# Signs of weights from scaled words in PSUM, and a pair's maxima split in PSUM

## The chip, the cores and the metric

The kernel runs on one core of one Trainium2 chip. The metric is device time in microseconds (us), the median of several runs. TensorE (PE) multiplies, VectorE (DVE), ScalarE (ACT) and GpSimd (POOL) do elementwise work, SyncE (SP) and ACT issue DMAs. Each engine works through its own instructions in order; semaphores order the engines among each other. SBUF is the working memory, PSUM the memory that matmuls write to, in eight banks.

## The reference

```
mask   = (q_bucket[..., :, None] == k_bucket[..., None, :])     # buckets: six sign bits of q @ proj, k @ proj
scores = where(mask, (q @ k.T) / 8, -1e9)                        # 2 batches x 8 heads, 768 x 768, head_dim 64
attn   = exp(scores - max(scores)); attn /= (sum(attn) + 1e-9)
x      = (attn @ v), heads joined: 1536 tokens x 512
h      = x @ w_in;  x = (s * relu(h)**2 + b) @ w_out             # first layer, 512 -> 2048 -> 512
h      = x @ w_in2; out = (h * clip(h + 3, 0, 6) / 6) @ w_out2   # second layer
```

All inputs are float32. The kernel receives the four weight matrices as 64-bit words (each float widened to a double, read as two 32-bit words), and makes float32 words of them on the chip.

## The kernel before, in words

The queries are cut into four units (two batches, two halves of 384 queries), each with four pairs of heads: 16 pairs, numbered g. For a pair, `qk` makes six tiles of scores twice (128 queries against 384 keys), and `smax` (line 473, DVE) reduces each to its negated row maximum, in two columns per slot. Masking is part of the product: key bits scaled by 2^100 push pairs of different buckets far down, so a row without any partner shows a maximum beyond 2^99. `both` (line 477) joins the two halves, `nx_split` (lines 483 to 486) clears such rows, adds a constant, splits the sum into a high and a low part and makes a flag, all into columns of `cols`; `nx_mm` (line 491, PE) transposes `cols` through a PSUM bank; `rows_in` (line 497, DVE) writes the rows into QA; `u_rows` (line 502, ACT) copies the rows with the flags out of the same bank. Then `st` makes the transposed scores with the maxima included, `texp` their exponentials, `t_hi` and `t_lo` (ACT, POOL) split these into two halves of 16 bits, `pv_mm`, `den_mm`, `recip`, `r_mm`, `x_scale`, `x_hi` and `x_lo` give the pair's part of x. Keys and queries are split in the same way (`k_hi` on ACT; `k_lo`, line 358, on POOL).

The two layers are eight jobs, one per layer and unit. A job has 32 weight tiles of 128x512: 16 for the first product (whose results pass `g_relu`, `g_prod`, `g_hi` and `g_lo` into G), 16 for the second. Each tile is split into a high part (`w_hi`, line 658, ACT) and a low part (`w_lo`, line 664, POOL), and takes 12 matmuls (line 688).

The first job of each layer also converts the weights, tile by tile: `w_load` brings 128x1024 words; `w_exp` (line 624, ACT) scales the upper words by 2^-112 into a PSUM bank, `wm`; `w_ends` with half 0 (line 636, ACT) writes the lower 16 bits of the new words, with half 1 (line 638, DVE) their upper 16 bits, which are the sign alone; `w_join` (line 643, DVE) shifts the scaled words left by three and joins them in. Then the tile is stored for the later jobs of the layer. The two conversions run from about 80 to 250 us and from about 360 to 463 us; attention of later pairs runs beside them.

The order on every engine comes from a planner (class `Plan`): each step is added with an engine, a due time, an estimated duration, what it needs, and which buffers of which ring it takes and gives back. The planner goes forward through the steps and picks, on each engine, the one that is due first among those that can start. A step's estimate or a ring's holder that changes can change the whole order. Rings that matter here: `S` with two PSUM banks (score tiles, and from pair 4 on the small products of a pair, that of `nx_mm` among them), `mm` with one PSUM bank (`wm`, and the small products of pairs 0 to 3).

Of the kernel before, what the change touches and what calls it, by code (L numbers as in the profile page):

```python
# [8 lines left out]
F32 = mybir.dt.float32  # L9
F32R = mybir.dt.float32r  # L10
# [11 lines left out]
NQ = 384  # L22
# [204 lines left out]
def attn_moe_moe2(ctx, tc, qT, kT, vT, proj, cvec, eye, w1_in, w1_out, w2_in, w2_out, out):  # L227
# [48 lines left out]
    cols = [const.tile([128, 114], F32R, name=f"cols{e}") for e in range(2)]  # L276
# [192 lines left out]
    def smax(s, j):  # L469
        g, c = divmod(s, SPP)  # L470
        if c == 0 and j == 0:
            pd[g]["nh"] = sm_p.tile([128, 2, SPP], F32, tag="nh", name="nh")
        nc.vector.reduce_max(out=pd[g]["nh"][:, j, c:c + 1], in_=sd.pop((s, j))[:, 0:NQ], axis=AX.X, negate=True)  # L473

    def both(g):
        pd[g]["nx"] = sm_p.tile([128, SPP], F32, tag="nx", name="nx")
        nc.vector.tensor_tensor(out=pd[g]["nx"], in0=pd[g]["nh"][:, 0], in1=pd[g]["nh"][:, 1], op=ALU.min)

    def nx_split(g):

# [256 lines left out]
    def o_store(j, d, key):  # L737
# [7 lines left out]
                 "vt": 4, "iv": 4, "pvs": 1, "U": 1, "ds": 1, "kH": 1, "qD": 1, "kHx": 1, "qDx": 1, "nx": 3, "nh": 2, "cols": 2, "fl": 1,  # L745
# [37 lines left out]
    for g in range(NP):  # L783
# [85 lines left out]
    for jn, (m, j, n) in enumerate(jobs):  # L869
        t0, dt = M[jn]  # L870
        prev = [("mm", jn - 1, 28 + f // 4) if jn else None for f in range(16)]
        for i in range(32):
            key = (jn, i)
            t = t0 + i * dt
            if jn == first[m]:
# [5 lines left out]
                    rel=[(wr, ck, 3)])  # L881
# [3 lines left out]
                add("DVE", tw, 0.66, w_join, (ck,), needs=[("we",) + ck, ("wd", 1) + ck], gives=[("wf",) + ck],  # L885
# [100 lines left out]
```

## Time and profile before

| | |
|---|---|
| runs | 907.68, 904.6, 899.4 us; median 904.6 |
| profiled execution | 901.18 us; span from first to last instruction 899.3 us, mean granted clock 0.971 |
| PE matmul / weight load, busy | 836.7 us (93%) / 741.4 us (82%) |
| DVE, ACT, POOL, busy | 497.8 us (55%), 590.5 us (66%), 574.5 us (64%) |
| the chain that ended last | PE 78%, DVE 12%, ACT 3%, DMA 3% |

Busy shares are means over stages that differ. The chain is followed back from the last instruction: at each step to what released it, or to the instruction before it on its engine. A wait of PE for DVE names the line that came last. "Granted clock" is the share of TensorE's full speed that the chip granted in a stretch.

### The profile page before, as it was taken

The numbers are of one execution on the slowest core, as the hardware profiler recorded it, in microseconds if no ns is written. First come the engines' busy times: TensorE is split into PE (matmuls) and PEld (weight loads), VectorE is DVE, ScalarE is ACT, GpSimd is POOL, SyncE is SP. The second block draws the span as 40 slices with busy tenths as digits, with TensorE's granted clock in tenths as the row PEclk, the third lists the DMA queues.
The fourth block names the chain that finished last, engine by engine and source line by source line (L and its number), as shares of the span: only waits on it lengthen the run. The fifth ranks groups of instructions, "written<-read, shape, count | busy, mean of one in ns | idle before, by whom it ended". The sixth has DMA issues, their size and how long they took to land.

```text
span 899.3 us, 15265 instructions
## 1 busy us (share of the span) xinstructions
PE 836.7 (93%) x5430; PEld 741.4 (82%) x5430; DVE 497.8 (55%) x852; ACT 590.5 (66%) x993; POOL 574.5 (64%) x388
## 2 busy tenths in 40 slices
PE   6689889779999999988999999999999999999998
PEld 2456569568887889977978997999998788999998
DVE  8577777887757673789544433540465542530520
ACT  4368769696875963899876636663588464753752
POOL 5467645684786856455778658566588665665664
PEclk9688899898999999999999999999999999999999
DMA  8858443566557666878966443444334222444442
GB/s 191 139 99 241 115 134 123 178 194 206 191 168 190 145 157 163 259 246 257 284 201 180 130 123 92 144 129 122 114 103 117 77 65 86 125 128 122 128 139 74
DMA packets 74988, 136.73 MB, mean 152 GB/s; under 512 B 20288, under 2 KB 30880, under 8 KB 74912
## 3 DMA queue, kind: packets, MB, share of 16 engines
q1 hardware_dynamic: 73088, 132.15, 51.4%
q10 hardware_dynamic: 1824, 3.60, 1.8%
q8 instruction: 43, 0.70, 0.3%
q14 instruction: 33, 0.27, 0.1%
HBM read 103.86 MB, written 21.54 MB: 139 GB/s over the span
## 4 chain that ended last, share of the span: by engine, by line
PE 78%; DVE 12%; ACT 3%; DMA 3%; issue 2%; SPq 0%; DVEq 0%; ACTq 0%
PE mm L688 55%; PE T L525 6%; PE S L465 6%; PE pv L554 5%; DVE wf L638 2%; DVE nh L473 2%; PE S L565 2%; DMA KA<-bits 1%; PE pv L586 1%; PE S L381 1%; DVE wf L643 1%; ACT P L531 1%; DVE QA L497 1%; DMA qD<-q_t 1%; PE pv L374 1%
## 5 line engine op out<-in xcount | busy, mean ns | idle before, releaser
L664 POOL TENSOR_TENSOR wl<-wf,wh 128x512 fp32r<-128x512 f32 x256 | 331.3, 1296 | 218.3 <-ACT wh L658 187.0
L688 PE MATMUL mm<-G,wh 128*128 128x384 f32 x1024 | 270.8, 346 | 6.2 <-DVE G L720 4.8
L688 PE MATMUL mm<-X,wh 128*128 128x384 f32 x1024 | 265.0, 339 | 10.7 <-DVE G L723 6.1
L658 ACT CAST wh<-wf 128x512 fp32r<-128x512 f32 x256 | 158.3, 618 | 111.1 <-PE mm L688 70.7
L544 POOL TENSOR_TENSOR pt<-P,pt 128x768 f16<-128x768 f32 x96 | 160.1, 1671 | 69.4 <-ACT pt L538 62.8
L688 PEld LDWEIGHTS mm<-X,wh 128*128 128x128 f32 x1024 | 183.1, 188 | 22.4 <-DVE G L723 9.8
L688 PEld LDWEIGHTS mm<-G,wh 128*128 128x128 f32 x1024 | 184.6, 190 | 18.5 <-issue 11.0
L688 PE MATMUL mm<-G,wl 128*128 128x384 f32 x512 | 173.8, 339 | 0.3 <-POOL wl L664 0.3
L688 PE MATMUL mm<-X,wl 128*128 128x384 f32 x512 | 171.8, 336 | 0.0
L473 DVE TENSOR_REDUCE nh<-S 128x1 f32<-128x384 f32 x192 | 104.2, 552 | 84.3 <-PE S L465 83.7
L531 ACT ACTIVATE P<-T 128x768 f32<-128x768 f32 x96 | 77.8, 810 | 39.5 <-PE T L525 34.3
L688 PEld LDWEIGHTS mm<-G,wl 128*128 128x128 f32 x512 | 96.9, 189 | 0.6 <-POOL wl L664 0.6
L688 PEld LDWEIGHTS mm<-X,wl 128*128 128x128 f32 x512 | 96.2, 188 | 0.3 <-POOL wl L664 0.3
L465 PE MATMUL S<-KA,QA 76*128 76x384 f32 x192 | 73.9, 385 | 15.1 <-DVE nh L473 9.1
L538 ACT CAST pt<-P 128x768 f16<-128x768 f32 x96 | 79.8, 834 | 7.4 <-PE pv L554 3.8
L525 PE MATMUL T<-QA,KA 108*128 108x384 f32 x192 | 71.1, 370 | 5.2 <-DVE QA L497 4.9
L525 PE MATMUL T<-QB,KB 128*128 128x384 f32 x192 | 68.7, 358 | 0.0
L465 PE MATMUL S<-KB,QB 128*128 128x384 f32 x192 | 68.0, 354 | 0.0
L465 PEld LDWEIGHTS S<-KA,QA 76*128 76x128 f32 x192 | 38.2, 199 | 31.8 <-DVE nh L473 14.4
L554 PE MATMUL pv<-pt,vt 128*64 128x384 f16 x576 | 61.8, 337 | 1.5 <-POOL pt L544 1.0
L638 DVE TENSOR_SCALAR wf<-wr 128x512 uint16<-128x512 uint16 x64 | 59.3, 926 | 6.5 <-DMA wr<-w_in 5.9
L358 POOL TENSOR_TENSOR KB<-kH,KA 64x1536 fp32r<-64x1536 f32 x14 | 48.8, 3487 | 13.6 <-ACT KA L352 13.4
(356 smaller groups left out, 985.9 us busy)
## 6 DMA issues: line engine op xcount, KB each, us to landing
wf<-w SPq DMA_DIRECT2D x187, 256.0 KB
wr<-w_in SPq DMA_DIRECT2D x32, 512.0 KB
w<-wf SPq DMA_DIRECT2D x64, 256.0 KB
wr<-w_out SPq DMA_DIRECT2D x32, 512.0 KB
KB<-KA SPq DMA_DIRECT2D x15, 384.0 KB
kH<-k_t SPq DMA_DIRECT2D x14, 384.0 KB
qD<-q_t SPq DMA_DIRECT2D x28, 192.0 KB
U<-ur SPq DMA_DIRECT2D x16, 192.0 KB
```

The costliest lines, as they stand in the source:

```text
L358: nc.gpsimd.tensor_tensor(out=operand(g, "KB")[0:64], in0=pd[g]["k"], in1=operand(g, "KA")[0:64].bitcast(F32), op=ALU.subtract)
L465: nc.tensor.matmul(out=sp[:, 0:NQ], lhsT=operand(g, Q)[0:n, h, 128 * t:128 * t + 128], rhs=operand(g, K)[0:n, h, NQ * j:NQ * j + NQ], star ...
L473: nc.vector.reduce_max(out=pd[g]["nh"][:, j, c:c + 1], in_=sd.pop((s, j))[:, 0:NQ], axis=AX.X, negate=True)
L525: nc.tensor.matmul(out=tp[:, j, 0:NQ], lhsT=operand(g, K)[0:n, h, c:c + 128], rhs=operand(g, Q)[0:n, h], start=(a == 0), stop=(a == 1))
L531: nc.scalar.activation(out=P, in_=td.pop((g, k))[:, :, 0:NQ], func=AF.Exp, scale=0.125)
L538: (nc.scalar.copy if THI(g) == "ACT" else nc.vector.tensor_copy)(pd[g][h][:, 0, 2 * i:2 * i + 2], pd[g]["P", k])
L544: e.tensor_tensor(out=pt[:, 1, 2 * i:2 * i + 2], in0=pd[g].pop(("P", k)), in1=pt[:, 0, 2 * i:2 * i + 2], op=ALU.subtract)
L554: nc.tensor.matmul(out=d["pv"][64 * h:64 * h + 64, 0:NQ], lhsT=vt[:, vc, 64 * h:64 * h + 64], rhs=d[h][:, a, c], start=(c == 0 and n == 0) ...
L638: nc.vector.tensor_scalar(out=f16[:, :, 1], in0=r16[:, :, 3], scalar1=0x8000, scalar2=None, op0=ALU.bitwise_and)
L658: nc.scalar.copy(hi.rearrange("p a b -> p (a b)"), wq[key]["wf"])
L664: nc.gpsimd.tensor_tensor(out=lo.rearrange("p a b -> p (a b)"), in0=d["wf"], in1=d["hi"].rearrange("p a b -> p (a b)").bitcast(F32), op=AL ...
L688: nc.tensor.matmul(out=a, lhsT=w[:, k, :], rhs=src[k][:, xi, :], start=(k0 + k == 0 and p == 0), stop=(k0 + k == nk - 1 and p == 2))
```

## The change

The sign is no longer taken from the loaded words in SBUF with a 16-bit instruction. `w_low` (before: `w_ends`, half 0) now writes whole 32-bit words with the lower 16 bits as value; `w_sign` takes the sign bit of the scaled words in PSUM and joins it to them; `w_join` follows. So the sign now needs both ACT instructions, and a loaded tile is given back by ACT alone. For a pair, the maxima go into a fixed buffer of three columns per slot, the third a constant 2^99; one reduction takes the least of the three into PSUM, and two instructions, not five, follow it there in place of `both` and `nx_split`. Rows without a partner are no longer cleared; their flag is made from the transposed rows by `u_rows`, which moves from ACT to DVE. `nx_split` now takes the PSUM bank that `nx_mm` took, and the planner's entries say so.

```diff
-    cols = [const.tile([128, 114], F32R, name=f"cols{e}") for e in range(2)]
+    cols = [const.tile([128, 108], F32R, name=f"cols{e}") for e in range(2)]
+    maxima = [const.tile([128, 3, SPP], F32, name=f"nh{e}") for e in range(2)]
...
-        nc.vector.reduce_max(out=pd[g]["nh"][:, j, c:c + 1], in_=sd.pop((s, j))[:, 0:NQ], axis=AX.X, negate=True)
-
-    def both(g):
-        pd[g]["nx"] = sm_p.tile([128, SPP], F32, tag="nx", name="nx")
-        nc.vector.tensor_tensor(out=pd[g]["nx"], in0=pd[g]["nh"][:, 0], in1=pd[g]["nh"][:, 1], op=ALU.min)
+        nc.vector.reduce_max(out=maxima[g % 2][:, j, c:c + 1], in_=sd.pop((s, j))[:, 0:NQ], axis=AX.X, negate=True)
 
     def nx_split(g):
 
-        nx, c = pd[g]["nx"], cols[g % 2]
-        mk = sm_p.tile([128, SPP], F32, tag="mk", name="mk")
-        nc.vector.scalar_tensor_tensor(out=mk, in0=nx, scalar=2.0 ** 99, in1=nx, op0=ALU.is_lt, op1=ALU.mult)
-        nc.vector.tensor_scalar(out=c[:, 96:102], in0=mk, scalar1=LN, scalar2=None, op0=ALU.add)
-        nc.vector.scalar_tensor_tensor(out=c[:, 102:108], in0=mk, scalar=LN, in1=c[:, 96:102].bitcast(F32), op0=ALU.add, op1=ALU.subtract)
-        nc.vector.tensor_scalar(out=c[:, 108:114], in0=nx, scalar1=2.0 ** 99, scalar2=None, op0=ALU.is_ge)
+
+        t, c = bank(g), cols[g % 2]
+        nx = t[:, 128:128 + SPP]
+        nc.vector.tensor_reduce(out=nx, in_=maxima[g % 2].rearrange("p j s -> p s j"), axis=AX.X, op=ALU.min)
+        nc.vector.tensor_scalar(out=c[:, 96:102], in0=nx, scalar1=LN, scalar2=None, op0=ALU.add)
+        nc.vector.scalar_tensor_tensor(out=c[:, 102:108], in0=nx, scalar=LN, in1=c[:, 96:102].bitcast(F32), op0=ALU.add, op1=ALU.subtract)
+        pd[g]["nr"] = t
...
     def u_rows(g):
         fl = raw_p.tile([128, 128], F32, tag="fl", name="fl")
-        nc.scalar.copy(fl[96:114], pd[g]["nr"][96:114, 0:128])
+        nc.vector.tensor_scalar(out=fl[96:102], in0=pd[g]["nr"][96:102, 0:128], scalar1=2.0 ** 99, scalar2=None, op0=ALU.is_ge)
...
-            nc.scalar.activation(out=f16[:, :, 0], in_=r16[:, :, 1], func=AF.Copy, scale=2.0 ** -13, bias=2.0 ** -14 - 0.5)
-        else:
-            nc.vector.tensor_scalar(out=f16[:, :, 1], in0=r16[:, :, 3], scalar1=0x8000, scalar2=None,
-                                    op0=ALU.bitwise_and)
+    def w_low(key):
...
+        nc.scalar.activation(out=d["wf"], in_=r16[:, :, 1], func=AF.Copy, scale=2.0 ** -13, bias=2.0 ** -14 - 0.5)
+
+    def w_sign(key):
+        d = wq[key]
+        nc.vector.scalar_tensor_tensor(out=d["wf"], in0=d["mt"], scalar=-2147483648, in1=d["wf"], op0=ALU.bitwise_and,
+                                       op1=ALU.bitwise_or)
...
-                for h in range(2):
-                    add("DVE" if h else "ACT", tw, 0.85 if h else 0.67, w_ends, (ck, h), needs=[("wr",) + ck] + ([("wd", 0) + ck] if h else before("wi", jn, i)),
-                        acq=[] if h else [("wf", ck)], gives=[("wd", h) + ck] + ([] if h else [("wi",) + ck]), rel=[(wr, ck, 3)])
+                add("ACT", tw, 0.65, w_low, (ck,), needs=[("wr",) + ck] + before("wi", jn, i),
+                    acq=[("wf", ck)], gives=[("wd",) + ck, ("wi",) + ck], rel=[(wr, ck, 2)])
+                add("DVE", tw, 0.69, w_sign, (ck,), needs=[("we",) + ck, ("wd",) + ck], gives=[("wg",) + ck])
```

The planner then orders everything anew. Three places of the order follow; names and lines are those of each kernel.

On DVE, the split of pair 5 (in the stretch 160 to 172 us of the profile), before and now:

```order
L473 TENSOR_REDUCE nh<-S 128x1 x2
L477 TENSOR_TENSOR nx<-nh 128x6
L705 SCALAR_TENSOR_TENSOR mm<-mm,cv,r__1906 128x384
L483 SCALAR_TENSOR_TENSOR mk<-nx 128x6
L484 TENSOR_SCALAR cols_143<-mk 128x6
L485 SCALAR_TENSOR_TENSOR cols_143<-mk,cols_143 128x6
L486 TENSOR_SCALAR cols_143<-nx 128x6
L638 TENSOR_SCALAR wf<-wr 128x512
L497 TENSOR_TENSOR QA_152<-S,eyes 12x768
L643 SCALAR_TENSOR_TENSOR wf<-wm,wf 128x512
```

```order
L479 TENSOR_REDUCE S<-nh_145 128x6
L480 TENSOR_SCALAR cols_143<-S 128x6
L481 SCALAR_TENSOR_TENSOR cols_143<-S,cols_143 128x6
L631 SCALAR_TENSOR_TENSOR wf<-wm,wf 128x512
L636 SCALAR_TENSOR_TENSOR wf<-wm,wf 128x512
L491 TENSOR_TENSOR QA_154<-S,eyes 12x768
L713 SCALAR_TENSOR_TENSOR G_1382<-mm,cv,G_1382 128x384
L698 SCALAR_TENSOR_TENSOR mm<-mm,cv,r__1887 128x384
L496 TENSOR_SCALAR fl<-S 6x128
```

Five instructions ahead of the transposition have become three (479 to 481), sign and join of a weight tile (631, 636) stand between them and the rows for QA (491), and the flag (496) comes two instructions after these, in the same PSUM tile S.

On ACT, in the conversion of the second matrix (wm: scaled words, r: relu, G: upper half, wh: upper half of a weight tile), before and now:

```order
L636 ACTIVATE wf<-wr 128x512
L624 ACTIVATE wm<-wr 128x512
L714 CAST G_1364<-mm 128x384
L658 CAST wh<-wf 128x512
L699 ACTIVATE r__4536<-mm,three 128x384
L658 CAST wh<-wf 128x512
L636 ACTIVATE wf<-wr 128x512
L624 ACTIVATE wm<-wr 128x512
```

```order
L618 ACTIVATE wm<-wr 128x512
L627 ACTIVATE wf<-wr 128x512
L532 CAST pt<-P 128x768
L692 ACTIVATE r__4511<-mm,three 128x384
L651 CAST wh<-wf 128x512
L618 ACTIVATE wm<-wr 128x512
L707 CAST G_1378<-mm 128x384
L627 ACTIVATE wf<-wr 128x512
L692 ACTIVATE r__4547<-mm,three 128x384
```

The scaling (624, now 618) always followed the low half (636, now 627); now it precedes it in some tiles, directly or with an instruction of G between.

On SP at the start, from the shift of pair 1's keys on (before, ACT issued `KA_151<-bits`, the key bits of pair 1, after the transpose in the planner's order), before and now:

```order
L355 DMA KB_153<-KA_151 64x1536
L342 DMA qD<-q_t 64x2x384 x2
L348 DMA vP<-v_t 128x768
L451 DMA_TRANSPOSE vt<-vhl 128x12x128
L406 DMA QA_152<-bits 12x384 x2
```

```order
L356 DMA KB_155<-KA_153 64x1536
L335 DMA kHx<-k_t 64x1536
L356 DMA KB_162<-KA_160 64x1536
L415 DMA KA_153<-bits 12x384 x4
L403 DMA kb_118<-bits 128x384
L343 DMA qDx<-q_t 64x2x384 x2
L407 DMA QA_154<-bits 12x384 x2
L349 DMA vP<-v_t 128x768
L452 DMA_TRANSPOSE vt<-vhl 128x12x128
```

The key and query bits of pair 1 (KA_153, QA_154) now stand ahead of the first transpose, on SP; two more loads of keys and shifts stand ahead of them.

## Rows read from the trace of the kernel before

**Rows 1.** Busy time by stage: window, length, engines in us (instructions), granted clock, DMA.

```profile
core 0: us, PE busy (x) PEld busy (x) DVE busy (x) ACT busy (x) POOL busy (x), PEclk, DMA share, GB/s
60.00:112.00 52.00, 43.21 (x362) 31.64 (x359) 41.88 (x65) 40.85 (x59) 37.40 (x21) 0.87 0.63 166
160.00:205.00 45.00, 32.60 (x212) 25.84 (x209) 38.62 (x51) 33.33 (x54) 32.80 (x19) 0.90 0.61 174
205.00:260.00 55.00, 55.00 (x406) 45.47 (x405) 37.15 (x68) 42.95 (x71) 35.89 (x23) 0.96 0.61 197
373.00:440.00 67.00, 59.26 (x321) 55.26 (x321) 55.55 (x95) 61.52 (x112) 37.25 (x28) 1.00 0.83 260
760.00:899.00 139.00, 135.99 (x779) 135.66 (x777) 41.42 (x71) 72.66 (x136) 81.08 (x63) 1.00 0.39 119
```

**Rows 2.** What PE waited for: releaser, us in total, times, longest us.

```profile
PE S L465 <- DVE nh L473: 9.1, 8, 3.3
PE mm L688 <- DVE G L720: 8.2, 7, 4.4
PE mm L688 <- DVE G L723: 7.6, 8, 1.5
PE S L491 <- DVE cols L486: 7.1, 3, 4.8
```

**Rows 3.** Timeline 165 to 170 us: start, us, engine, line; idle before, releaser.

```profile
165.71 3.42 POOL L358 TENSOR_TENSOR KB<-kH,KA 64x1536 fp32r<-64x1536 f32 x1
165.76 3.39 DVE L485 SCALAR_TENSOR_TENSOR cols<-mk,cols 128x6 fp32r<-128x6 f32 x1
...
169.29 0.77 PE L491 MATMUL S<-eyes,cols 128*114 128x128 f32 x2 [4.76 <-DVE cols L486]
```

**Rows 4.** Timeline 196 to 205 us.

```profile
196.35 3.48 POOL L358 TENSOR_TENSOR KB<-kH,KA 64x1536 fp32r<-64x1536 f32 x1
...
197.54 5.80 DVE L638 TENSOR_SCALAR wf<-wr 128x512 uint16<-128x512 uint16 x1
...
199.80 3.22 POOL L544 TENSOR_TENSOR pt<-P,pt 128x768 f16<-128x768 f32 x2
...
204.36 1.01 PE L688 MATMUL mm<-G,wh 128*128 128x384 f32 x2 [4.44 <-DVE G L720]
```

**Rows 5.** DVE lines one by one: duration in ns, min/median/max; first and last start.

```profile
L485 DVE SCALAR_TENSOR_TENSOR cols<-mk,cols x16: 165/166/3387, 31.1 to 726.4; 128x6 fp32r<-128x6 f32 x16
L638 DVE TENSOR_SCALAR wf<-wr x64: 395/774/5802, 80.3 to 458.3; 128x512 uint16<-128x512 uint16 x64
L643 DVE SCALAR_TENSOR_TENSOR wf<-wm,wf x64: 668/691/694, 82.7 to 462.4; 128x512 int32<-128x512 int32 x64
L720 DVE SCALAR_TENSOR_TENSOR G<-mm,cv,G x64: 519/618/618, 132.2 to 798.3; 128x384 fp32r<-128x384 f32 x64
```

**Rows 6.** Line 638 alone in two stretches: window, length, DVE busy us (calls).

```profile
160.00:205.00 45.00, 11.51 (x7) 0.90 0.61 174
373.00:425.00 52.00, 13.03 (x16) 1.00 0.80 251
```

**Rows 7.** The chain that ended last, 90 to 100 us: start, us, what.

```profile
95.30 1.35 DVE nx L477
...
96.67 1.66 DVE mk L483
```

**Rows 8.** Timeline 19 to 36 us.

```profile
23.08 12.41 ACTq L414 DMA_DIRECT2D KA<-bits  x4
...
35.39 0.66 PE L465 MATMUL S<-KA,QA 76*128 76x384 f32 x1 [5.54 <-DMA KA<-bits]
```

**Rows 9.** ACT lines: shape xcount, busy us, mean ns; idle before, releasers.

```profile
L658 ACT CAST wh<-wf 128x512 fp32r<-128x512 f32 x256 | 158.3, 618 | 111.1 <-PE mm L688 70.7 <-POOL wl L664 25.3 <-DVE wf L643 9.4
L636 ACT ACTIVATE wf<-wr 128x512 uint16<-128x512 uint16 x64 | 51.0, 797 | 0.1
L624 ACT ACTIVATE wm<-wr 128x512 f32<-128x512 f32 x64 | 41.5, 648 | 6.2 <-DVE wf L643 6.2
L714 ACT CAST G<-mm 128x384 fp32r<-128x384 f32 x64 | 30.7, 480 | 3.6
```

More of the change, by code (lines that the diff above doesn't have):

```diff
@@ L470, in smax @@
         g, c = divmod(s, SPP)
-        if c == 0 and j == 0:
-            pd[g]["nh"] = sm_p.tile([128, 2, SPP], F32, tag="nh", name="nh")
-        nc.vector.reduce_max(out=pd[g]["nh"][:, j, c:c + 1], in_=sd.pop((s, j))[:, 0:NQ], axis=AX.X, negate=True)
-    def both(g):
-        pd[g]["nx"] = sm_p.tile([128, SPP], F32, tag="nx", name="nx")
-        nc.vector.tensor_tensor(out=pd[g]["nx"], in0=pd[g]["nh"][:, 0], in1=pd[g]["nh"][:, 1], op=ALU.min)
-    def nx_split(g):
-        nx, c = pd[g]["nx"], cols[g % 2]
-        mk = sm_p.tile([128, SPP], F32, tag="mk", name="mk")
-        nc.vector.scalar_tensor_tensor(out=mk, in0=nx, scalar=2.0 ** 99, in1=nx, op0=ALU.is_lt, op1=ALU.mult)
-        nc.vector.tensor_scalar(out=c[:, 96:102], in0=mk, scalar1=LN, scalar2=None, op0=ALU.add)
-        nc.vector.scalar_tensor_tensor(out=c[:, 102:108], in0=mk, scalar=LN, in1=c[:, 96:102].bitcast(F32), op0=ALU.add, op1=ALU.subtract)
-        nc.vector.tensor_scalar(out=c[:, 108:114], in0=nx, scalar1=2.0 ** 99, scalar2=None, op0=ALU.is_ge)
+        nc.vector.reduce_max(out=maxima[g % 2][:, j, c:c + 1], in_=sd.pop((s, j))[:, 0:NQ], axis=AX.X, negate=True)
+    def nx_split(g):
+        t, c = bank(g), cols[g % 2]
[4 more added lines that the diff above has]
+        pd[g]["nr"] = t
     def nx_mm(g):
-        t = bank(g)
-        nc.tensor.matmul(out=t[0:114, 0:128], lhsT=cols[g % 2].bitcast(F32), rhs=ident, start=True, stop=True)
-        pd[g]["nr"] = t
+        nc.tensor.matmul(out=pd[g]["nr"][0:108, 0:128], lhsT=cols[g % 2].bitcast(F32), rhs=ident, start=True, stop=True)
     def rows_in(g):
@@ L501, in u_rows @@
         fl = raw_p.tile([128, 128], F32, tag="fl", name="fl")
-        nc.scalar.copy(fl[96:114], pd[g]["nr"][96:114, 0:128])
+        nc.vector.tensor_scalar(out=fl[96:102], in0=pd[g]["nr"][96:102, 0:128], scalar1=2.0 ** 99, scalar2=None, op0=ALU.is_ge)
         pd[g]["fl"] = fl
     def u_out(g):
-        queue[0].dma_start(out=urow[g], in_=pd[g]["fl"][108:114])
+        queue[0].dma_start(out=urow[g], in_=pd[g]["fl"][96:102])
     def u_in(g):
@@ L829, in attn_moe_moe2 @@
         allmx = [("mx", SPP * g + i, j) for i in range(SPP) for j in range(2)]
-        add("DVE", A[SPP * g + SPP - 1] + 1.9, 0.12, both, (g,), needs=allmx, acq=[("nx", g)], gives=[("mx", g)], rel=[("nh", g)])
         a, dt = A[SPP * g + SPP - 1], (A[SPP * g + SPP - 1] - A[SPP * g]) / (SPP - 1)
-        add("DVE", a + 2.0, 0.7, nx_split, (g,), needs=[("mx", g)], acq=[("cols", g)], gives=[("nc", g)], rel=[("nx", g)])
-        add("PE", a + 2.8, 0.3, nx_mm, (g,), needs=[("nc", g)], acq=[(br, ("n", g))], gives=[("nt", g)], rel=[("cols", g)])
+        add("DVE", a + 2.0, 0.7, nx_split, (g,), needs=allmx, acq=[("cols", g), (br, ("n", g))], gives=[("nc", g)], rel=[("nh", g)])
+        add("PE", a + 2.8, 0.3, nx_mm, (g,), needs=[("nc", g)], gives=[("nt", g)], rel=[("cols", g)])
         add("DVE", a + 3.2, 0.95, rows_in, (g,), needs=[("nt", g)] + free, gives=[("mi", g)], rel=[(br, ("n", g), 2)])
-        add("ACT", a + 3.2, 0.25, u_rows, (g,), needs=[("nt", g)], acq=[("fl", g)], gives=[("nm", g)], rel=[(br, ("n", g), 2)])
+        add("DVE", a + 4.2, 0.2, u_rows, (g,), needs=[("nt", g)], acq=[("fl", g)], gives=[("nm", g)], rel=[(br, ("n", g), 2)])
         add("DMA", a + 8.0, (0.4, 0.1), u_out, (g,), needs=[("nm", g)], gives=[("uo", g)], rel=[("fl", g)])
@@ L929, in attn_moe_moe2 @@
             nc.vector.memset(c.bitcast(F32), 0.0)
+        for c in maxima:
+            nc.vector.memset(c[:, 2], 2.0 ** 99)
         for fn, a, on in plan.order():
```

16 lines of the change are left out of this document (6 added, 10 removed).

## The prediction

> **What bounds the kernel now.** I read the stages first, then what TensorE (PE) waits for, then the stretches where its waits are longest. In the stage table the last stage is simply full: 136.0 us of 139, at a granted clock of 1.00, which is the upper of its two levels, 2.4 GHz [rows 1]. Nothing in this change can shorten it. The losses lie earlier. From 60 to 112 us PE is idle for 8.8 us and its clock is 0.87; from 160 to 205 it is idle for 12.4 us at 0.90, and the next 55 us still run at 0.96; from 373 to 440 it is idle for 7.7 us. In the first two of these VectorE (DVE) is the fullest elementwise engine (41.9 us of 52, 38.6 of 45), in the third ScalarE (ACT) is at 61.5 and DVE at 55.6 of 67 [rows 1].
>
> PE's longest waits all name DVE: 9.1 us for the row maxima, 8.2 and 7.6 for the lower half of G in the two matrices, 7.1 for `cols` [rows 2].
>
> Why is DVE late? The timeline shows it. At 165.76 the instruction of line 485, on 128x6 elements, takes 3.39 us, and ends within 0.02 us of a GpSimd (POOL) instruction that started 0.05 us before it (165.71 + 3.42 = 169.13). PE stands still for 4.76 us and then multiplies `cols` [rows 3]. At 197.54 line 638 takes 5.80 us, while POOL runs one instruction after another until 203.0; PE waits 4.44 us [rows 4]. The spread of each line's durations separates two kinds. Wholly in SBUF are line 485, with a median of 0.17 us and a maximum of 3.39, and line 638, 0.40 at best and 5.80 at worst. Lines 643 and 720 read one operand from PSUM and never exceed 0.69 and 0.62 us in 64 calls each [rows 5]. So a DVE instruction wholly in SBUF can be held until POOL pauses, and one with a PSUM operand is not. The change puts a PSUM operand into every instruction that replaces a blocked one.
>
> The Trainium skill (SBUF, "Who interferes with whom") says that the two engines share a port pair as an exclusive lock for a whole instruction. By that rule line 638 would have had the pair at 199.8, when the first POOL instruction ended, and have taken about 2.7 us in all; its 5.80 us go beyond it. The sum below would be the same by the rule and by the row, since it takes PE's measured wait.
>
> **The change, part by part.** I count what PE gets back, not what DVE saves; a DVE saving is worth at most the PE idle behind it.
>
> *Maxima and split.* Five instructions per pair become three. None of the new three is wholly in SBUF; each should stay near the 0.17 us of an unblocked line 485 [rows 5], with gaps about 0.8 us a pair. PE waited 7.1 us for `cols` [rows 2]; I take **6**. Bounds: 3.5 (only the one wait of 4.76 shrinks, and by all but 1.3) and 7.1.
>
> *The sign, first weight matrix.* Line 638 becomes an instruction of the same kind as line 643, so 0.69 us each. The 5.80 us call shrinks by 5.1 us, and PE's 4.44 us behind it go. Of the other 3.8 us waited for line 720 I take 1. Together **5.4**; bounds 4.4 and 8.2.
>
> *The sign, second matrix.* From 373 to 425 us line 638 averages 13.03 / 16 = 0.81 us, against 11.51 / 7 = 1.64 from 160 to 205 [rows 6]. The 32 tiles save 32 x 0.12 = 3.9 us of DVE, and I take two thirds as lying ahead of the lower half of G: **2.6**; bounds 0 and 7.6, the whole wait for line 723.
>
> *First stage.* At 95.3 and 96.7 us lines 477 and 483 take 1.35 and 1.66 us on the chain [rows 7], against 0.17 unblocked: **2.7**. Bounds 0 and the stage's idle of 8.8.
>
> *The clock.* From 160 to 260 us the clock below 1.00 costs 32.6 x 0.10 + 55.0 x 0.04 = 5.5 us of full-speed work [rows 1]. It is low in and after the stretch with most idle; with most of that gone I take half, **2.7**; bounds 0 and 5.5.
>
> *Start of the program.* The planner reorders everything. Before, the four DMAs with the key bits of pair 1 are issued from ACT after SP's transpose; those four issues last 12.41 us, and PE waits 5.54 [rows 8]. Now they stand on SP ahead of the transpose, and the bits of pairs 2 and 3 come behind it, when PE has two pairs to work on. I take **3**; bounds 5.5 saved, and 5.5 lost if the same hole opens at pair 2.
>
> *What is added.* The split takes its PSUM bank from the reduction on, where the matmul took it before, and `u_rows` (now on DVE; between 0.17 and 0.62 us by lines 485 and 720 [rows 5], I take 0.3) gives it back after `rows_in` and sometimes two or three instructions more: about 2 us longer, while the score tiles have one bank of two. Line 465 waits 9.1 us now [rows 2]; I charge **2**, bounds 0 and 4. The sign now needs the scaled words, so their bank is held 0.69 us longer per tile: I charge **1.5**, bounds 0 and the 29 of the rival below. ACT loses 16 copies, and `w_low` writes dense words: between 0.80 (line 636 now) and 0.62 (line 658) [rows 9]; I take 0.72, nearer to line 636 because its strided input stays, 64 x 0.08 = 5 us. I cost that at nothing: where ACT is fullest, PE's wait names DVE. If ACT were the limit there, half of it would be gained. The two added memsets of 18 columns lie beside the first DMAs.
>
> **Sum:** 6 + 5.4 + 2.6 + 2.7 + 2.7 + 3 - 2 - 1.5 = 18.9 us off the profiled execution's 901.2 (span 899.3 and 1.9 around it): 882.3. That execution lies 3.4 us below the median of 904.6; carried over, **886**. All good bounds together, 42.7 us, would give 862; all bad ones, the 29 among them, 935.
>
> **Rivals.**
>
> *More comes back* (chance 0.12). If nearly every wait for DVE goes, the good bounds of the maxima, the two signs and the first stage give 7.1 + 8.2 + 7.6 + 8.8, and the rest as taken 2.2: 33.9 us less, 871 in the median, between 864 and 875. For it: one cause stands behind most of the waits. Against: the maxima themselves and `rows_in` remain in DVE's queue.
>
> *Nothing comes back* (0.16). The order is fixed in advance; where DVE is in time, PE waits for the next late one: ACT at 61.5 of 67 us, or POOL, which keeps its instruction of 3.4 us. The waits would change their names: 896 to 910. Against: in the two longest waits nothing but DVE was outstanding.
>
> *The bank of the scaled words becomes the bound; slower* (0.07). Place: from 373 us, one bank, one tile at a time. It was held for the scaling (0.65, line 624) and the join (0.69). Now the sign is added and, where the new order puts the low half behind the scaling on ACT, an instruction of G (0.48, line 714) and 0.72: 0.65 + 0.48 + 0.72 + 0.69 + 0.69 = 3.2 us and gaps [rows 5, 9]. A tile comes every 52 / 16 = 3.25 us [rows 6]. It decides when the hold passes that: ACT then stands at the next scaling, with PE's relu behind it. At 0.9 us over for 32 tiles that is 29 us, less the 18 gained outside this stage: 912, with the 3.4 us 916. Against: only some tiles have that order, and they are prepared up to seven ahead.
>
> *The slower kind of instruction decides* (0.03). Where POOL leaves room line 638 needs 0.40 us; now it always needs 0.69. Were all 64 calls such, DVE would gain 64 x 0.29 = 18.6 us of work; a fifth of it on the path gives 4 us, 909 in the median. The measured total speaks against it: 11.51 us for 7 calls where the new kind needs 4.8 [rows 6]. The Trainium skill (VectorE: DVE Perf Modes, "Why PSUM operands drop a tier") says that an operand in PSUM costs such an instruction its faster mode; line 638's best call agrees, its mean does not.
>
> *It does not do what it says* (in the second rival's chance). The new sign still has one operand in SBUF and could be held as before. Line 643 has the same kinds of operands and is never held [rows 5].
>
> **From these to the numbers.** My forecast has 0.62, with its own range 875 to 895. Faster by over 1% means under 895.6, and 1% is about what a measurement of this kernel can tell from no change: 0.62 + 0.12 = 0.74. Within 1%: 0.16 + 0.03 = 0.19. Slower: 0.07. The range 869 to 903 leaves out the slower rival, the upper part of "nothing" with the slower kind, and the best third of "more": 2 in 10.
>
> **What would show it.** The sign's 64 calls all within 0.67 to 0.72 us, and the three instructions on 128x6 with maxima under 0.5 us: the mechanism. PE's waits for `cols` under 2 us in all, no wait of 4 us for the lower half of G, and a clock above 0.95 in the stretch that answers to 160 to 205: the terms of the maxima, the first sign and the clock. PE's first pairs without a gap of 5 us: the start. I am wrong if those spreads shrink and PE's idle in the three stretches, 8.8 + 12.4 + 7.7 = 28.9 us, does not fall by 12 or more; if the scaling on ACT waits for the join by much more than its 6.2 us now [rows 9], it is the bank.

## The result, and the profile after

The changed kernel took 875.46 us (median of 4 runs, 873.28 to 876.93); the kernel before 903.93 (4 runs, the three ahead of the prediction among them). The ratio is 0.9685, 95% interval 0.9635 to 0.9735: 28.5 us faster, where 18.9 were forecast. The profiled execution of after has a span of 875.1 us against 899.3. Three executions of the experiments below (one of before in another order, two of the kernel before in the last series) took over 1.5% longer than the fastest of their kernel, and are left out of the medians here as they are of the ratios.

**Did the instructions come free?** The rows of after that answer to [rows 5], the mapping of the weights first (631 is the sign, 636 the join, 627 the low half on ACT), then the maxima of a pair (479 to 481, twelve pairs in a score bank, four in another bank), `u_rows` (496), a split of G (713), and the low half of v (445). Columns: duration in ns, min/median/max; first and last start.

```profile
L631 DVE SCALAR_TENSOR_TENSOR wf<-wm,wf x64: 628/691/694, 74.9 to 449.0; 128x512 int32<-128x512 int32 x64
L636 DVE SCALAR_TENSOR_TENSOR wf<-wm,wf x64: 672/691/693, 76.0 to 449.7; 128x512 int32<-128x512 int32 x64
L627 ACT ACTIVATE wf<-wr x64: 642/665/714, 71.5 to 448.3; 128x512 int32<-128x512 uint16 x64
L479 DVE TENSOR_REDUCE S<-nh x12: 171/182/183, 111.6 to 701.7; 128x6 f32<-128x18 f32 x12
L480 DVE TENSOR_SCALAR cols<-S x12: 164/164/166, 111.8 to 701.9; 128x6 fp32r<-128x6 f32 x12
L481 DVE SCALAR_TENSOR_TENSOR cols<-S,cols x12: 164/165/166, 112.0 to 702.1; 128x6 fp32r<-128x6 f32 x12
L496 DVE TENSOR_SCALAR fl<-S x12: 286/296/298, 117.2 to 705.0; 6x128 f32<-6x128 f32 x12
L445 DVE SCALAR_TENSOR_TENSOR vhl<-vP,sc,vhl x8: 918/1320/3270, 19.3 to 302.3; 128x768 f16<-128x768 f32 x8
```

The sign's longest call fell from 5.80 us to 0.69, its total from 59.3 to 43.9 us although its best call went up from 0.395; the small instructions have no spread left. Line 445, still wholly in SBUF and untouched by the change, is still held, up to 3.27 us.

**Where TensorE's time went.** The answer to [rows 1], in stretches of about equal work: the borders are 60 us and the first, 193rd, 385th, 769th, 1153rd and 2305th product of the layers (two stretches a weight pass, then longer ones). Columns as there.

```profile
0.00:60.00 60.00, 40.92 (x182) 22.66 (x182) 45.66 (x89) 30.25 (x35) 36.77 (x20) 0.87 0.75 166
60.00:101.80 41.80, 39.17 (x367) 29.73 (x363) 32.76 (x61) 34.26 (x52) 27.84 (x17) 0.95 0.53 165
101.80:190.70 88.90, 81.16 (x599) 66.76 (x597) 66.47 (x125) 74.80 (x127) 62.66 (x38) 0.98 0.61 183
190.70:261.20 70.50, 70.50 (x512) 59.97 (x511) 50.29 (x88) 58.24 (x92) 54.47 (x35) 1.00 0.69 204
261.20:354.30 93.10, 86.21 (x524) 78.18 (x523) 44.77 (x82) 49.19 (x89) 51.23 (x37) 0.95 0.59 156
354.30:457.50 103.20, 96.22 (x578) 88.07 (x577) 74.32 (x131) 90.56 (x160) 66.73 (x47) 0.98 0.77 248
457.50:739.50 282.00, 282.00 (x1923) 257.80 (x1922) 110.04 (x198) 170.52 (x293) 192.75 (x135) 1.00 0.41 116
739.50:875.10 135.60, 132.23 (x763) 131.91 (x762) 39.87 (x68) 71.15 (x134) 79.83 (x62) 1.00 0.40 121
```

Length minus PE busy is PE's idle time. The same for before, between its own borders at 60, 112.3, 204.9, 279.1, 371.0, 471.9 and 763.5 us, first three rows of its view and then both kernels in a table:

```profile
0.00:60.00 60.00, 41.94 (x175) 24.50 (x176) 40.11 (x81) 27.66 (x34) 30.58 (x18) 0.80 0.79 150
60.00:112.30 52.30, 43.51 (x363) 31.94 (x360) 42.18 (x66) 41.15 (x59) 37.40 (x21) 0.87 0.63 165
112.30:204.90 92.60, 75.50 (x508) 63.56 (x507) 75.12 (x116) 70.64 (x119) 57.79 (x36) 0.95 0.50 153
```

| stretch | idle before | idle after | clock before | clock after |
|---|---|---|---|---|
| start to 60 us | 18.1 | 19.1 | 0.80 | 0.87 |
| 60 us to the first product | 8.8 | 2.6 | 0.87 | 0.95 |
| products 1 to 192 | 17.1 | 7.7 | 0.95 | 0.98 |
| products 193 to 384 | 0 | 0 | 0.97 | 1.00 |
| products 385 to 768 | 2.3 | 6.9 | 1.00 | 0.95 |
| products 769 to 1152 | 9.7 | 7.0 | 1.00 | 0.98 |
| products 1153 to 2304 | 3.4 | 0 | 1.00 | 1.00 |
| the rest | 3.3 | 3.4 | 1.00 | 1.00 |
| whole span | 62.6 | 46.7 | | |

The span fell by 24.2 us: 15.9 of idle, and 8.3 of busy time (836.7 to 828.4 us) for the same 5430 multiplications, which is the clock. The rest of the 28.5 is how the profiled executions stand to the medians. One stretch, products 385 to 768, got worse by 4.6 us of idle and a lower clock.

PE's waits, the answer to [rows 2] (releaser, us in total, times, longest):

```profile
PE S L466 <- DVE nh L472: 10.4, 9, 2.8
PE mm L681 <- DVE G L713: 6.8, 5, 2.7
PE mm L681 <- DVE G L716: 6.4, 7, 2.8
PE small L382 <- DMA projb<-proj_: 5.3, 1, 5.3
PE S L466 <- DMA QA<-bits: 3.5, 1, 3.5
```

The wait for `cols` is gone; no wait for G exceeds 2.8 us. Those for the maxima and for the two splits of G stay, at other places. The longest for line 713 lies in the stretch that got worse, here in the timeline of after (start, us, engine, line; idle before, releaser; x2 marks two instructions in a row):

```profile
285.59 0.94 DVE L425 TENSOR_REDUCE am<-vP 128x1 f32<-128x768 f32 x1
...
287.08 0.94 DVE L434 TENSOR_REDUCE vm<-vP 128x1 f32<-128x768 f32 x1
...
288.06 0.15 DVE L435 TENSOR_SCALAR vm<-vm 128x1 f32<-128x1 f32 x1
288.13 1.13 DVE L713 SCALAR_TENSOR_TENSOR G<-mm,cv,G 128x384 fp32r<-128x384 f32 x2
...
288.79 0.61 PE L681 MATMUL mm<-X,wh 128*128 128x384 f32 x2 [2.67 <-DVE G L713]
```

The whole scaling of a v block, 285.59 to 288.21, is one step for the planner and stands ahead of the split of G that PE needs. None of it is held: it is plain queueing. The same again at 301.9 us (1.84).

On ACT, the answer to [rows 9] (shape, count, busy us, mean ns; idle before):

```profile
L627 ACT ACTIVATE wf<-wr 128x512 int32<-128x512 uint16 x64 | 42.8, 668 | 0.1
...
L618 ACT ACTIVATE wm<-wr 128x512 f32<-128x512 f32 x64 | 40.6, 635 | 7.1 <-DVE wf L636 4.0 <-DMA wr<-w_in 3.0
```

The scaling waits for the join for 4.0 us, less than the 6.2 before. The low half takes 0.67 us where the strided write took 0.80.

### The profile page after: what moved, and what is told of

Its sections match the earlier page's. It is cut to its first block, busy times and chain, and to the rows that moved or that the text cites. A ratio compares the mean times of both kernels' runs of the same rounds, so it can differ in the third digit from the quotient of the medians.

```text
span 875.1 us, 15178 instructions
## 1 busy us (share of the span) xinstructions
PE 828.4 (95%) x5430; PEld 735.1 (84%) x5430; DVE 464.2 (53%) x838; ACT 579.0 (66%) x977; POOL 572.3 (65%) x388
## 4 chain that ended last, share of the span: by engine, by line
PE 80%; DVE 7%; DMA 5%; ACT 4%; issue 2%; POOL 1%; SPq 1%; ACTq 0%; DVEq 0%; POOLq 0%
PE mm L681 58%; PE T L519 6%; PE S L466 6%; PE pv L548 6%; DMA kH<-k_t 2%; PE S L559 1%; DMA wr<-w_in 1%; PE S L382 1%; DMA vP<-v_t 1%; PE pv L580 1%; DVE nh L472 1%; DVE wf L631 1%; ACT wf L627 1%; DVE am L425 1%; DVE KA L330 1%
## 5 line engine op out<-in xcount | busy, mean ns | idle before, releaser
L681 PE MATMUL mm<-G,wh 128*128 128x384 f32 x1024 | 265.5, 340 | 0.0
L681 PEld LDWEIGHTS mm<-X,wh 128*128 128x128 f32 x1024 | 186.0, 191 | 23.9 <-DVE G L713 9.8
L681 PEld LDWEIGHTS mm<-G,wh 128*128 128x128 f32 x1024 | 182.6, 188 | 11.4 <-issue 10.4
L681 PE MATMUL mm<-X,wl 128*128 128x384 f32 x512 | 173.7, 339 | 0.0
L681 PE MATMUL mm<-G,wl 128*128 128x384 f32 x512 | 171.5, 335 | 0.0
L525 ACT ACTIVATE P<-T 128x768 f32<-128x768 f32 x96 | 78.0, 812 | 49.3 <-PE T L519 46.8
L466 PE MATMUL S<-KA,QA 76*128 76x384 f32 x192 | 72.8, 379 | 14.2 <-DVE nh L472 10.4
L519 PE MATMUL T<-QA,KA 108*128 108x384 f32 x192 | 69.0, 359 | 3.4 <-ACT pt L532 1.2
L519 PE MATMUL T<-QB,KB 128*128 128x384 f32 x192 | 65.7, 342 | 0.0
L466 PEld LDWEIGHTS S<-KA,QA 76*128 76x128 f32 x192 | 37.4, 195 | 31.2 <-DVE nh L472 21.1
L631 DVE SCALAR_TENSOR_TENSOR wf<-wm,wf 128x512 int32<-128x512 int32 x64 | 43.9, 686 | 33.2 <-ACT wf L627 26.7
```

What stands on the lines that cost most here:

```text
L466: nc.tensor.matmul(out=sp[:, 0:NQ], lhsT=operand(g, Q)[0:n, h, 128 * t:128 * t + 128], rhs=operand(g, K)[0:n, h, NQ * j:NQ * j + NQ], star ...
L519: nc.tensor.matmul(out=tp[:, j, 0:NQ], lhsT=operand(g, K)[0:n, h, c:c + 128], rhs=operand(g, Q)[0:n, h], start=(a == 0), stop=(a == 1))
L525: nc.scalar.activation(out=P, in_=td.pop((g, k))[:, :, 0:NQ], func=AF.Exp, scale=0.125)
L631: nc.vector.scalar_tensor_tensor(out=d["wf"], in0=d["mt"], scalar=-2147483648, in1=d["wf"], op0=ALU.bitwise_and, op1=ALU.bitwise_or)
L681: nc.tensor.matmul(out=a, lhsT=w[:, k, :], rhs=src[k][:, xi, :], start=(k0 + k == 0 and p == 0), stop=(k0 + k == nk - 1 and p == 2))
```

## The experiments

**Theory A**: the time goes to VectorE instructions wholly in SBUF that are held while GpSimd runs; freeing them is the gain. **Theory B**: the planner, given new costs, found a better order, and the kinds of instruction matter little. **Theory C**: there are simply fewer VectorE instructions per pair. The planner reorders all engines whenever a step changes, so most runs fix either the order or the kinds. The runs came in three series, each on one chip; the base of each ratio is the kernel before in the same series. In what follows, an instruction is "held" where it takes much longer than the shortest call of its line.

### Each part alone, with an order of its own

The sign alone (before's maxima kept), and the pair alone (before's weight mapping kept):

```diff
-            nc.vector.tensor_scalar(out=f16[:, :, 1], in0=r16[:, :, 3], scalar1=0x8000, scalar2=None,
-                                    op0=ALU.bitwise_and)
+        nc.vector.scalar_tensor_tensor(out=d["wf"], in0=d["mt"], scalar=-2147483648, in1=d["wf"], op0=ALU.bitwise_and,
+                                       op1=ALU.bitwise_or)
```

> The kernel before with the sign taken from PSUM, the pairs' maxima and their split as before; the planner orders anew. Theory A (VectorE was held by GpSimd in instructions wholly in SBUF, and the change frees it): the first sign's 5.4 us, 2.6 of the second and about half of the clock's 2.7 and of the start's 3 come back, 888 to 895 us; the lines of the pair keep maxima above 1.5 us. Theory B (the planner's new order made the gain, whatever the instructions): anything between 875 and 910, with no tie to these terms.

```diff
-        nc.vector.tensor_tensor(out=pd[g]["nx"], in0=pd[g]["nh"][:, 0], in1=pd[g]["nh"][:, 1], op=ALU.min)
...
+        nx = t[:, 128:128 + SPP]
+        nc.vector.tensor_reduce(out=nx, in_=maxima[g % 2].rearrange("p j s -> p s j"), axis=AX.X, op=ALU.min)
```

> The kernel before with the pairs' maxima and split as in the change, the sign taken from SBUF as before; the planner orders anew. Theory A: the maxima's 6 us, the first stage's 2.7 and a part of the clock come back, 890 to 897 us; PE's waits for cols are gone, the sign keeps calls above 3 us and with them waits for the lower half of G of 2 us and more. Theory B: anything between 875 and 910.

The sign alone: 897.33 us, ratio 0.9963 (0.9923 to 1.0002), no gain that can be told from none, and a miss. The pair alone: 889.07 us, 0.9873 (0.9814 to 0.9932), 1 us below the expected range. In the first the maxima were held as before, and PE waited 6.9 and 5.0 us for `cols`. In the second PE still waited 2.2 us for `cols`, where none was expected, and no wait for G exceeded 1.3 us, where 2 and more were expected, though the sign was held:

```profile
L632 DVE TENSOR_SCALAR wf<-wr x64: 450/1120/4532, 64.9 to 454.7; 128x512 uint16<-128x512 uint16 x64
```

The two gains, 3.5 (not clear of none) and 11.8 us, make 15.3; both parts together gave 28.5, and 23.5 in the last series. Each part has an order of its own here, so this alone doesn't tell the parts from the order.

### The changed kernel's order, with old kinds

The order of steps on each engine is that of after, word for word. For the maxima only an operand moves back to SBUF:

```diff
-        nx = t[:, 128:128 + SPP]
+        nx = sm_p.tile([128, SPP], F32, tag="nx", name="nx")
```

> The changed kernel in its own order, with the pair's least value kept in SBUF instead of PSUM, so that two of the three instructions are wholly in SBUF; nothing else differs. Theory A: those two are held in some of 16 calls (maxima over 1.5 us), and 4 to 9 us are lost: 879 to 884. Theory C (it was the count, five instructions to three, and not the place): 874 to 877, as the change.

For the sign the old VectorE instruction comes back, and with it the strided write of the low half on ACT (0.79 us a call in this run, 0.67 in after); one more buffer of raw words is there, as they are read later:

```diff
-        nc.scalar.activation(out=d["wf"], in_=r16[:, :, 1], func=AF.Copy, scale=2.0 ** -13, bias=2.0 ** -14 - 0.5)
+        nc.scalar.activation(out=d["f16"][:, :, 0], in_=r16[:, :, 1], func=AF.Copy, scale=2.0 ** -13, bias=2.0 ** -14 - 0.5)
...
-        nc.vector.scalar_tensor_tensor(out=d["wf"], in0=d["mt"], scalar=-2147483648, in1=d["wf"], op0=ALU.bitwise_and,
-                                       op1=ALU.bitwise_or)
+        nc.vector.tensor_scalar(out=d["f16"][:, :, 1], in0=d["r16"][:, :, 3], scalar1=0x8000, scalar2=None,
+                                op0=ALU.bitwise_and)
```

> The changed kernel in its own order, with only the sign as the old 16-bit instruction in SBUF (low half 16-bit on ACT, one more buffer of loaded words); the pair's instructions stay in PSUM. Theory A: the sign is held in some of 64 calls (maximum over 3 us) and 8 to 14 us are lost, 883 to 890, as between the two runs before this one (912.9 less 900.8). If the sign mattered only while the pair's instructions were held too: under 880.

And both edits together:

> The changed kernel in its own order on every engine, but with the sign as the old 16-bit instruction in SBUF (the low half as the old 16-bit one on ACT, one more buffer of loaded words) and the three instructions of the pair in SBUF instead of PSUM. Theory A: the calls are held again (maxima over 3 us in the sign, over 1.5 in the pair's lines), and at least 15 of the 28 us are lost: 890 to 905. Theory B: the order is the same, so 873 to 880.

Pair in SBUF: 900.77 us, ratio 1.0001 (0.9968 to 1.0034). Sign in SBUF: 902.74, 1.0023 (0.9987 to 1.0058). Both: 912.92, 1.0135 (1.0074 to 1.0196). All three lie above the range that theory A gave: the direction is the one it gave, the size is a miss each time. The pair in SBUF is the clean case: one operand's place, in 16 pairs, took back the whole gain, and the number of instructions is that of after, so theory C falls. Theory B falls as well: this order with the old kinds is slower than before, by about 1%. In the two runs with the old sign the slower write on ACT has a share in the loss that no run tells apart. Here is the pair in SBUF, first its three lines, then its waits:

```profile
L479 DVE TENSOR_REDUCE nx<-nh x16: 156/174/178, 37.6 to 722.3; 128x6 f32<-128x18 f32 x16
L480 DVE TENSOR_SCALAR cols<-nx x16: 171/572/5469, 37.8 to 722.5; 128x6 fp32r<-128x6 f32 x16
L481 DVE SCALAR_TENSOR_TENSOR cols<-nx,cols x16: 165/1188/4666, 38.0 to 724.0; 128x6 fp32r<-128x6 f32 x16
```

```profile
PE S L486 <- DVE cols L481: 12.0, 7, 5.2
...
PE T L519 <- DVE QA L491: 5.5, 4, 2.2
...
PE small L486 <- DVE cols L481: 3.6, 2, 3.0
```

And one such hold in its timeline:

```profile
50.99 3.46 POOL L359 TENSOR_TENSOR KB<-kH,KA 64x1536 fp32r<-64x1536 f32 x1 [0.41 <-ACT KA L353]
...
52.23 0.17 DVE L479 TENSOR_REDUCE nx<-nh 128x6 f32<-128x18 f32 x1
...
52.43 5.25 DVE L480 TENSOR_SCALAR cols<-nx 128x6 fp32r<-128x6 f32 x1
...
54.42 3.23 POOL L538 TENSOR_TENSOR pt<-P,pt 128x768 f16<-128x768 f32 x2
...
57.72 0.17 DVE L481 SCALAR_TENSOR_TENSOR cols<-nx,cols 128x6 fp32r<-128x6 f32 x1
...
57.94 0.76 PE L486 MATMUL small<-eyes,cols 128*108 128x128 f32 x2 [3.02 <-DVE cols L481]
```

Line 538 stands there for two instructions in a row, of 1.6 us each. The hold ends 0.03 us after the second of them does (54.42 + 3.23 = 57.65, 52.43 + 5.25 = 57.68), as POOL pauses for 0.08 us. It need not be a pause, though. Near the end of the same run:

```profile
722.32 1.65 POOL L538 TENSOR_TENSOR pt<-P,pt 128x768 f16<-128x768 f32 x1 [0.97 <-ACT pt L532]
...
722.54 1.46 DVE L480 TENSOR_SCALAR cols<-nx 128x6 fp32r<-128x6 f32 x1
723.93 1.27 POOL L657 TENSOR_TENSOR wl<-wf,wh 128x512 fp32r<-128x512 f32 x1
```

Here the hold ends at 724.00, as line 538 ends and with the next POOL instruction already begun. Of the 15 calls over 0.9 us of lines 480 and 481, all end 0.02 to 0.03 us after the end of a POOL instruction; four lasted over more than one such end, and five ended with the next one begun. In before, the 14 such calls of lines 477 to 486 all ended with the first. So the prediction's "until POOL pauses" fits line 638 at 197.54 and is too strong as a rule; what lets an instruction in at one end and not at another is not shown.

PE waits 15.6 us for `cols` where after waits none. With the sign in SBUF:

```profile
L633 DVE TENSOR_SCALAR wf<-wr x64: 392/478/6261, 75.5 to 471.5; 128x512 uint16<-128x512 uint16 x64
```

```profile
PE mm L683 <- DVE G L715: 11.5, 7, 4.5
```

The Trainium skill (SBUF, "Who interferes with whom") says that `tensor_reduce` never contends with GpSimd on this chip, and that `tensor_scalar` can. The two lines agree: 178 ns at worst in 16 calls, one of them while POOL ran at 52.23, against 5.47 us. So "wholly in SBUF" in theory A is too wide: the reduction is, and was not held. The Trainium skill also says there that the loser waits for a whole instruction of the winner; the hold at 52.43 lasted over the rest of one and two more, so the measurement goes beyond it.

### The order before, with new kinds

First the sign alone, in PSUM, directly ahead of the join, in before's order:

```diff
         wf = wq[key]["wf"]
+        nc.vector.scalar_tensor_tensor(out=wf, in0=wq[key]["mt"], scalar=-2147483648, in1=wf, op0=ALU.bitwise_and,
+                                       op1=ALU.bitwise_or)
```

> The kernel before, in its own order on PE, ACT, POOL and SP, with the sign taken from PSUM and put directly ahead of the join on VectorE, the one place where it always can run; nothing is planned anew, the pair's lines are as before. Theory A: the long calls go (5.8 us at 198 us), 4 to 9 us less than before, 892 to 897. Theory B: an old order with other instructions gains nothing or loses, as its places were chosen for others: 900 to 910.

903.1 us, ratio 1.0017 (0.9977 to 1.0056): a miss again. The maxima are still held there, up to 3.40 us a call, and the sign lost its place: before, it could run while ACT scaled the words, and only the join waited for them (21.1 us in all); now the sign does. That this is why the gain stays out is not tested. Idle of VectorE ahead of the sign, in this kernel:

```profile
DVE wf L637 <- ACT wm L624: 33.0, 18, 8.7
```

Then both parts, with the pair's four instructions (the flag among them) reading from spare columns of the last score bank, directly behind the last row maximum. The other engines keep their order; on VectorE the pair's instructions and the sign move, and the pair's are four instead of five:

```diff
+        if (c, j) == (SPP - 1, 1):
+            split(g, sp[:, NQ:NQ + SPP])
...
+        nc.vector.tensor_reduce(out=nx, in_=maxima[g % 2].rearrange("p j s -> p s j"), axis=AX.X, op=ALU.min)
+        nc.vector.tensor_scalar(out=c[:, 96:102], in0=nx, scalar1=LN, scalar2=None, op0=ALU.add)
+        nc.vector.scalar_tensor_tensor(out=c[:, 102:108], in0=nx, scalar=LN, in1=c[:, 96:102].bitcast(F32), op0=ALU.add, op1=ALU.subtract)
+        nc.vector.tensor_scalar(out=c[:, 108:114], in0=nx, scalar1=2.0 ** 99, scalar2=None, op0=ALU.is_ge)
```

> The kernel before with its order of work on TensorE, ScalarE, GpSimd and SyncE kept, and both parts of the change in their VectorE kinds alone: the sign taken from the scaled words in PSUM directly ahead of the join, and the pair's least value, the two addends and the flag taken from the last score bank in PSUM, directly behind the last row maximum. No VectorE instruction of the two parts has all its operands in SBUF. Theory A1, that the kinds bring the gain in any order: 880 to 890, that is most of the 11.8 us that the pair's part brought with its own order and some of the sign's; waits for the columns gone from TensorE's list. Theory A2, that an order tight enough to be hurt by a hold is needed as well: 895 to 903; waits for the columns gone, but as much time waited by TensorE for the join's operand (before, 8.2 + 7.6 us for the two g splits) and for the maxima. The largest time of the pair's small instructions should be under 0.5 us in both.

885.35 us, ratio 0.986 (0.9778 to 0.9942): in the middle of what the kinds alone should give, 12.6 us under the kernel before beside it (897.93). One of its small lines, and its longest waits for VectorE and for the query bits:

```profile
L479 DVE TENSOR_SCALAR cols<-S x16: 164/165/167, 31.4 to 712.6; 128x6 fp32r<-128x6 f32 x16
```

```profile
PE mm L685 <- DVE G L720: 8.4, 11, 1.5
PE S L465 <- DVE nh L472: 5.8, 6, 2.4
PE S L465 <- DMA QA<-bits: 5.7, 1, 5.7
...
PE S L465 <- DVE cols L481: 0.6, 2, 0.3
```

The wait for `cols` is down to 0.6 us, in an order that the change did not touch on any engine but VectorE.

### Other orders

Before and after, each planned anew with a latency of 0.21 instead of 0.20 us:

```diff
-    SAFE, LAT, DMA_LAT, SAME = 0.5, 0.2, 1.7, {"DVE": 0.1, "ACT": 0.1, "POOL": 0.1}
+    SAFE, LAT, DMA_LAT, SAME = 0.5, 0.21, 1.7, {"DVE": 0.1, "ACT": 0.1, "POOL": 0.1}
```

> The kernel before with one planner constant changed by 5% (the latency between engines, 0.20 to 0.21), so that it is ordered anew; the instructions are the same. It measures what a new order alone can do. Theory A: within 8 us of the kernel before, 893 to 909. Theory B, to explain the change: 885 or less must be within reach.

> The changed kernel with one planner constant, the latency between engines, at 0.21 instead of 0.20 us: the same instructions in another order. If the kinds of the instructions carry the gain and the order is one of many that do (theory A): 872 to 885. If the changed kernel's order is a lucky one (theory B): 890 to 900.

Before in another order: 908.0 us, ratio 1.0061 (1.0022 to 1.0101), with more waiting for `cols`, to which 4.8 us on a second tile come:

```profile
PE S L491 <- DVE cols L486: 19.3, 7, 5.8
```

After in another order: 867.11 us, 0.9673 (0.9588 to 0.9758), 5 us under the range that was expected. So the gain outlives its order, and the one new order without the new kinds that was tried gives none. Beside it on the same chip the changed kernel ran again:

> The changed kernel once more, beside the next one on the same chip: 872 to 880 by every theory.

874.41 us, ratio 0.9743 (0.9667 to 0.9819). Its four runs (870.14 to 876.96) lie all above the four of the other order (866.16 to 869.94), 7.3 us between the medians: that version was the faster one in this series, though the two intervals against before overlap.

### v in two steps

The multiply and the sum of v's scaling as two steps of the planner, so that a split of G can pass between them:

```diff
-            add("DVE", tv, 2.6, v_scale, (g,), needs=[("v", g)], acq=[("iv", g)], gives=[("vs", g)])
+            add("DVE", tv, 1.6, v_scale, (g,), needs=[("v", g)], acq=[("iv", g)], gives=[("vs", g)])
+            add("DVE", tv + 3.0, 1.1, v_sum, (g,), needs=[("vs", g)], gives=[("vm", g)], rel=[("vP", g, 2)])
```

> The changed kernel with the two reductions over a pair's v as two planner steps (1.6 and 1.1 us) in place of one of 2.6, ordered anew. In the changed kernel they stand twice between the two halves of G in the second job, and PE waits up to 2.7 us behind each. If those waits are the loss of that job (10.9 us over its work): 867 to 872. If they are only passed on to the next late engine: 873 to 880.

> The changed kernel with the scaling of v given to the planner as two steps (the multiply and the sum apart), so that a split of g need not wait behind both. If the two waits of 2.7 us for a g split behind v's scaling were on the path: 3 to 6 us less than the changed kernel on the same chip, about 871. If the time comes back in another wait: within 2 us of it.

871.22 us in one series, ratio 0.9682 (0.9605 to 0.9759); in the other 872.81, 0.9732 (0.9661 to 0.9803), beside 874.41 of the changed kernel: 1.6 us, and the runs overlap. No gain can be told. In the second trace a wait has taken the place of the old ones:

```profile
PE T L523 <- DVE QA L495: 5.8, 3, 3.6
...
PE mm L686 <- DVE G L718: 3.2, 2, 2.9
```

The rows of the maxima (line 495) cost 5.8 us, where after waits 0.2 for them.

## Why the prediction was right, and where its sizes were not

The forecast's mechanism held: the instructions that were held and now have a PSUM operand are held no longer, and putting one operand back brings the holds and the time back. Its size did not: 28.5 us against 18.9, and 875.46 lies only 0.5 us inside the forecast's own range. The table sets the profiled executions side by side (span minus PE busy is idle; busy time is for the same 5430 multiplications). Each row is one execution; the two of after differ by 2.8 us of idle and 2.7 of busy time.

| kernel | held | order | idle | PE busy |
|---|---|---|---|---|
| before | both | before's | 62.6 | 836.7 |
| sign freed | pair | before's | 61.8 | 841.9 |
| both freed | none | before's | 49.3 | 836.6 |
| after | none | after's | 46.7 | 828.4 |
| after, again | none | after's | 43.9 | 831.1 |
| pair in SBUF | pair | after's | 61.6 | 835.1 |
| sign in SBUF | sign | after's | 60.8 | 839.6 |
| both in SBUF | both | after's | 68.8 | 838.4 |

In before's order the kinds return 13.3 us of idle and nothing of the busy time. In after's order they return 22 to 25 of idle and 7 to 10 of busy time. So about half of the gain needs no new order of the other engines (12.6 of 23.5 us by the medians of the last series), and the other half comes only where unheld instructions meet the new order. Either half of the change missing costs all of it in that order.

Of idle the sum had 16.2 us (18.9 less the clock's 2.7), and 15.9 came. That it agrees so well is in part luck, as terms that were too small and too large cancel:

- *Maxima and split*, 6 us: somewhat low. The waits for `cols` went to none, from 7.1 us [rows 2] and 1.1 more on a second tile, which the prediction did not count; so the upper bound of 7.1 was passed. The three lines stay under 0.19 us. Before:

```profile
PE small L491 <- DVE cols L486: 1.1, 2, 0.9
```

- *The sign, first weight matrix*, 5.4: right in its place. Up to the 192nd product PE's wait for line 720 was 6.9 us, and is 1.8 now for 713. Over the whole kernel it fell only from 8.2 to 6.8, since from product 385 on it rose from 1.2 to 5.0, behind v's scaling. The prediction did not see that wait. Splitting the step left 3.2 to 6.9 us of it in the two runs, and brought another wait.
- *The sign, second matrix*, 2.6: too high. The waits for the second split fell from 7.6 to 6.4 us.
- *First stage*, 2.7: too low. Idle between 60 us and the first product fell from 8.8 to 2.6. I had priced two instructions on the chain; the waits for the maxima and their rows went too.
- *The clock*, 2.7: the term most mis-sized; busy time fell by 8.3 us. I had looked only at 160 to 260 us, but the start and the first stage ran at 0.80 and 0.87 and now run at 0.87 and 0.95. In the execution with both freed in the old order idle fell as well, and busy time did not: there the stretch from 60 us to the first product has a clock of 0.84. That execution was the slowest of its four, but the four together say the same: their median clock over the span is 0.976, against 0.977 of before and 0.982 of after in that series. Which feature of the new order brings the clock up is not settled.
- *Start of the program*, 3: did not come. The wait for the key bits went from 5.5 us to one of 3.5 for the query bits, but PE waits more for the maxima up to the first product (6.9 to 8.9), and idle to 60 us rose from 18.1 to 19.1. The sign that I had named for this term, no gap of 5 us at the first pairs, came true without the gain.
- *What is added*: 2 us were charged for the score bank; the wait for the maxima rose by 1.3 (9.1 to 10.4), from what cause is not shown. The bank of the scaled words cost nothing; the scaling waits less for the join than before, so that rival falls. ACT's low half took 0.67 us, not 0.72, and 42.8 us instead of 51.0 in all.

The idle in the stretches that answer to my three fell from 35.6 us to 17.3, more than the 12 I asked for. "Nothing comes back" is refuted by the time. "More comes back" named nearly this time, 871, but not for its reason: it wanted nearly every wait for DVE gone, and 23.6 us of waits for the maxima and for G remain. The slower kind of instruction did not decide: VectorE's busy time fell from 497.8 to 464.2 us.

## What to carry to other kernels

When the spread of a line's durations is wide on one engine and its long calls end together with instructions of another engine, change the kind of operand before the order; and free every instruction of that kind on the path, since those that stay can cost the whole gain. Price such a hold by the idle of the engine that waits, add what the clock returns for it as a term of its own, and expect the gain to depend on the order: test the new kind in the old order and the old kind in the new one before giving the credit to either.

## What the runs showed that I had not expected

- A hold can last over more than one POOL instruction: 5.25 us over the rest of one of 3.46 and two whole ones of 1.6. Long or short, the 15 holds of the pair's lines in that run each ended within 0.03 us after the end of a POOL instruction, whether POOL then paused or not.
- A reduction from SBUF to SBUF was not held in 16 calls (178 ns at most), right beside a `tensor_scalar` of a third of its elements that was held for 5.47 us.
- How little it takes: in a tight order 16 calls of two lines on 128x6 elements, 44 us busy instead of 5, took back the whole gain (900.77 us, ratio 1.0001).
